# Turning the local heads' queries and keys once, by pairs of tokens, with two copies of 64 partitions

## The chip, the cores and the metric

The kernel runs on one core of one Trainium2 chip. The metric is the device time in microseconds of one execution. A core has five engines with a queue of instructions each: TensorE (PE; its weight loads are listed apart, as PEld), VectorE (DVE), ScalarE (ACT), GpSimd (POOL) and SyncE (SP, which here issues loads). Each engine works through its own queue in order and waits on semaphores that the others raise.

## The reference, cut to what matters

```python
# attention: batch 4, 8 heads, 576 tokens, 64 values a head
rel = pos[:, None] - pos[None, :]
mask_local = (rel >= 0) & (rel < 32)                    # heads 0 to 3
mask_strided = (rel >= 0) & (pos[None, :] % 32 == pos[:, None] % 32)   # heads 4 to 7
scores = np.where(masks, scale * q @ k.T, -1e9)
attn = softmax(scores)
x = (attn @ v) as 2304 rows of 512
# mixture of experts: 8 experts, each row goes to the best one
logits = x @ w_gate; e = argmax; gate = softmax(logits)[e]
out = gate * (relu(x @ w1[e]) @ w2[e])
```

## The kernel before, in words

The kernel has two phases. In the first (some 130 us) the attention is worked out, the rows x are stored and each row's expert is found. In the second each expert's rows are gathered and multiplied with its weights, with TensorE busy almost without a gap.

The attention runs as a sequence of 25 steps written out by hand (`SEQ`): 16 units of the strided heads ("z") and 9 of the local heads ("l"). A unit passes through stages: A turns queries and keys (tokens on partitions) so that the 64 values of a head stand on partitions; B multiplies them to scores, and VectorE takes the row maximum (`mx`, `mxl`) and subtracts it; ScalarE exponentiates; C turns the weights (`tp`, `tpl`) and ScalarE copies them out (`ptz`, `ptl`); D multiplies with the values (`oz`, `ol`), and VectorE divides by the sums (`smz`, then `xz` or `xl`); E turns the result for the gate. One step of the loop issues C of unit i, A of i+3, B of i+2, E of i-1, D of i, so that each engine has the work of several units in its queue.

The change is in `l_a(c, gi)`, stage A of the local heads. A chunk c is one pair of heads of one batch; its loads `lk` and `lq` lie as 96 partitions with, for each of two heads h, 6 tokens g of 64 values d: token 6p+g stands on partition p. `KTL` and `QTL` want it turned: partition 64h+d, column 6p+g. `l_a` is called 16 times, twice for each of 8 chunks, and each call makes one PSUM tile `tl` for the keys and one for the queries. Eight calls stand alone in their step ("singles" below), the other eight come two by two ("pairs"). Which step has one is set by `la_target`. The tiles `tl` share the pool `ps_t` of three banks with `tq` (strided queries and keys), `tp`, `tpl`, `tx`, `txl` and `tg`: a fourth tile waits for the bank of the first to be copied out. For the first chunk, and in some other places, `fill` issues matmuls on a constant tile (`hot`) whose results are overwritten.

Of the kernel before, what the change touches and what calls it, by code (L numbers as in the profile page):

```python
# [42 lines left out]
LE = "ss"  # L43
# [10 lines left out]
def bc(ap, axis, n):  # L54

    a = ap.unsqueeze(axis)
    shape = list(a.shape)
    shape[axis] = n
    return a.to_broadcast(shape)
# [3 lines left out]
def kernel(  # L63
# [10 lines left out]
    nc = tc.nc  # L74
# [25 lines left out]
    ident = const.tile([128, 128], F32, name="ident")  # L100
# [31 lines left out]
    with ExitStack() as p1:  # L132
# [26 lines left out]
        def fill(t, c):  # L159

            p, w = t.shape
            for _ in range(FL.count(c) if c != "*" else 1): nc.tensor.matmul(t, lhsT=hot[:, 0:p], rhs=bc(hot, 1, w // 128) if w % 128 == 0 else bc(hot[:, 0:w // 4], 1, 4), start=True, stop=True)
# [5 lines left out]
        KTL = [cp.tile([128, S], F32, name=f"ktl{i}") for i in range(4)]  # L168
        VLL = [cp.tile([128, 18, 65], F32, name=f"vll{i}") for i in range(8)]
        QTL = [cp.tile([128, S], F32, name=f"qtl{i}") for i in range(4)]  # L170
# [250 lines left out]
        def l_a(c, gi):  # L421
            for src, nm in ((lk[c], "k"), (lq[c], "q")):
                t = ps_t.tile([128, 3, 96], F32, tag="t", name="tl")
                fill(t.rearrange("p a b -> p (a b)"), nm.upper())
                if c == 0:
                    for _ in range(XF[2 * gi + (nm == "q")]):
                        fill(t.rearrange("p a b -> p (a b)"), "*")
                for i in range(3):

                    f = src.rearrange("p h g d -> p (h g d)")  # L430
                    g = 64 * (3 * gi + i)
                    nc.tensor.transpose(t[:, i, :], f[:, 320 + g:448 + g], ident[:96, :96])
                    nc.tensor.transpose(t[0:64, i, :], f[:, g:g + 64], ident[:96, :96])
                dst = QTL if nm == "q" else KTL
                {"s": nc.scalar.copy, "v": nc.vector.tensor_copy}[LE[nm == "q"]](dst[c % 4].rearrange("d (p g) -> d p g", g=6)[:, :, 3 * gi:3 * gi + 3], t.rearrange("d g p -> d p g"))

        def l_b(vv):
            s = ps_s.tile([128, 2, 512], F32, tag="s", name="sl")
# [299 lines left out]
        def emit_la(m):  # L738
            while la_done[0] < m:
                i = la_done[0]  # L740
                assert la_ok(i)
                load_to("lq", i // 2)
                l_a(i // 2, i % 2)
                la_done[0] += 1
# [302 lines left out]
    with ExitStack() as p2:  # L1047
# [184 lines left out]
        t = pools["ps_w"].tile([128, 512], F32, tag="w", name="warm2")  # L1232
# [134 lines left out]
```

## Time and profile before

| | |
|---|---|
| median of 3 runs | 380.55 us (378.71 to 381.32) |
| the profiled execution: its time | 377.83 us |
| its span, first to last instruction | 376.1 us |
| so outside the span | 1.7 us |
| mean granted TensorE clock | 0.993 of 2.4 GHz |
| busy share of the span: PE, DVE, ACT, POOL | 94%, 60%, 44%, 29% |

The busy shares are means over two phases with different limits; what the change is worth is read from the first phase. The profiled execution was 2.7 us under the median, which is as much as the three runs spread.

### The profile page before, as it was taken

The page shows a single profiled execution, that of the slowest core. Times are in us where ns is not written, and L with a number is a line of the kernel's source. Part 1 is how long each engine was busy: PE and PEld are TensorE (multiplying, and loading weights), DVE is VectorE, ACT ScalarE, POOL GpSimd, SP SyncE. Part 2 cuts the span into 40 slices and gives each one's busy share as a digit, 9 for nine tenths or more (in the row PEclk, how much of TensorE's full clock was granted, in tenths as well). Part 3 has the DMA queues.
Part 4 walks back from the last instruction along what each step waited for, and adds up shares of the span by engine and source line. Part 5 has one row for each costly group of instructions (what it writes and reads, how often), then busy time and mean ns, then how long its engine had stood idle before and what let it go on. Part 6 is the DMA issues. An engine that isn't in the chain of part 4 may idle for free. (4 is left out here: it accounts for less than half of the span.)

```text
span 376.1 us, 11209 instructions
## 1 busy us (share of the span) xinstructions
PE 354.6 (94%) x4685; PEld 321.8 (86%) x4686; DVE 224.3 (60%) x492; ACT 165.0 (44%) x301; POOL 110.0 (29%) x166
## 2 busy tenths in 40 slices
PE   7789999799998978999999999999999999999993
PEld 4678887678886647999999999999999999988992
DVE  5445664654567778445655655476576576676651
ACT  2345554355553316243435435444435535545531
POOL 4011615101653133173144024125226025030502
PEclk9999999999999989999999999999999999999998
DMA  6789969694112168999465367367467476475301
GB/s 149 165 177 198 219 169 246 161 221 106 35 62 63 59 219 234 47 287 350 161 195 185 100 196 236 118 191 227 164 218 224 126 227 226 141 256 169 108 2 59
DMA packets 59630, 62.95 MB, mean 167 GB/s; under 512 B 26077, under 2 KB 45533, under 8 KB 59570
## 3 DMA queue, kind: packets, MB, share of 16 engines
q1 hardware_dynamic: 53938, 47.75, 46.6%
q0 software_dynamic: 5632, 14.39, 13.2%
q8 instruction: 39, 0.64, 0.8%
q14 instruction: 21, 0.17, 0.1%
HBM read 52.67 MB, written 9.60 MB: 166 GB/s over the span
## 5 line engine op out<-in xcount | busy, mean ns | idle before, releaser
L1100 PE MATMUL ph<-xh,w1h 128*128 128x280 f32 (+5 forms) x252 | 78.5, 312 | 0.0
L1102 PE MATMUL ph<-xh,w1l 128*128 128x280 f32 (+5 forms) x252 | 75.4, 299 | 0.0
L1101 PE MATMUL ph<-xl,w1h 128*128 128x280 f32 (+5 forms) x252 | 75.3, 299 | 0.0
L1117 ACT ACTIVATE hh<-ph 128x280 fp32r<-128x280 f32 (+5 forms) x64 | 26.8, 419 | 95.5 <-PE ph L1102 93.6
L1118 DVE SCALAR_TENSOR_TENSOR hl<-ph,hh 128x280 fp32r<-128x280 f32 (+5 forms) x64 | 29.8, 466 | 52.3 <-ACT hh L1117 52.1
L1146 POOL DMA_INDIRECT out_dram<-yo,routing x22 | 22.7, 1030 | 128.1 <-DVE yo L1171 99.9
L1101 PE MATMUL y<-hl,w2h 128*128 128x280 f32 (+4 forms) x192 | 58.6, 305 | 0.0
L1102 PE MATMUL y<-hh,w2l 128*128 128x280 f32 (+4 forms) x192 | 58.5, 305 | 0.0
L1100 PE MATMUL y<-hh,w2h 128*128 128x280 f32 (+4 forms) x192 | 58.4, 304 | 0.0
L1080 DVE TENSOR_TENSOR w1l<-w1r,w1h 128x1024 fp32r<-128x1024 f32 x31 | 38.0, 1226 | 17.8 <-ACT w1h L1079 12.4
L1100 PEld LDWEIGHTS ph<-xh,w1h 128*128 128x128 f32 x252 | 47.6, 189 | 0.4
L1101 PEld LDWEIGHTS ph<-xl,w1h 128*128 128x128 f32 x252 | 47.7, 189 | 0.2
L1102 PEld LDWEIGHTS ph<-xh,w1l 128*128 128x128 f32 x252 | 47.5, 189 | 0.0
L1080 DVE TENSOR_TENSOR w2l<-w2r,w2h 128x1024 fp32r<-128x1024 f32 x32 | 39.2, 1224 | 10.8 <-ACT w2h L1079 10.3
L1101 PEld LDWEIGHTS y<-hl,w2h 128*128 128x128 f32 x192 | 36.1, 188 | 0.3 <-DVE hl L1118 0.3
L1100 PEld LDWEIGHTS y<-hh,w2h 128*128 128x128 f32 x192 | 36.1, 188 | 0.0
L1102 PEld LDWEIGHTS y<-hh,w2l 128*128 128x128 f32 x192 | 36.1, 188 | 0.0
L1079 ACT CAST w1h<-w1r 128x1024 fp32r<-128x1024 f32 x31 | 32.2, 1040 | 3.8 <-DMA w1r<-in_moe_w_dram 3.8
L1079 ACT CAST w2h<-w2r 128x1024 fp32r<-128x1024 f32 x32 | 33.3, 1040 | 0.1
L1183 POOL DMA_INDIRECT gt<-g_dram,routing x22 | 23.4, 1065 | 15.4 <-DMA g_dram<-GA 9.0
L125 POOL DMA_INDIRECT xg<-x_dram,routing x19 | 21.3, 1121 | 22.2 <-PE px L1090 10.3
L408 POOL DMA_DIRECT2D x_dram<-xz x16 | 11.0, 694 | 53.2 <-DVE xz L388 46.7
(211 smaller groups left out, 636.9 us busy)
## 6 DMA issues: line engine op xcount, KB each, us to landing
w1r<-in_moe_w_dram SPq DMA_DIRECT2D x32, 512.0 KB
w2r<-in_moe_w_dram SPq DMA_DIRECT2D x32, 512.0 KB
zk<-in_k_dram SPq DMA_DIRECT2D x16, 144.0 KB
zq<-in_q_dram SPq DMA_DIRECT2D x16, 144.0 KB
vzs<-in_v_dram SPq DMA_DIRECT2D x32, 72.0 KB
lk<-in_k_dram SPq DMA_DIRECT2D x16, 144.0 KB
lq<-in_q_dram SPq DMA_DIRECT2D x16, 144.0 KB
x_dram<-xz POOLq DMA_DIRECT2D x16, 144.0 KB, 3.7
```

Of the source, the lines that this page charges most:

```text
L125: nc.gpsimd.indirect_dma_start(out=t[:r], out_offset=None, in_=x_dram[:, :], in_offset=bass.IndirectOffsetOnAxis(ap=idx[:r], axis=0),)
L408: nc.gpsimd.dma_start(out=x_dram[r0:r0 + S, c0:c0 + 128].rearrange("(p g) c -> p g c", g=16)[:, 8 * gh:8 * gh + 8, :], in_=xx[64 * b:64 * ...
L1079: nc.scalar.copy(hi, t)
L1080: nc.vector.tensor_tensor(lo, t, hi.bitcast(F32), op=ALU.subtract)
L1100: nc.tensor.matmul(o, lhsT=wh, rhs=xh, start=first, stop=False)
L1101: nc.tensor.matmul(o, lhsT=wh, rhs=xl, start=False, stop=False)
L1102: nc.tensor.matmul(o, lhsT=wl, rhs=xh, start=False, stop=last)
L1117: nc.scalar.activation(hh, o, AF.Relu)
L1118: nc.vector.scalar_tensor_tensor(hl, o, 0.0, hh.bitcast(F32), op0=ALU.max, op1=ALU.subtract)
L1146: s = nc.gpsimd.indirect_dma_start(out=out[:, :], out_offset=bass.IndirectOffsetOnAxis(ap=idx, axis=0), in_=o, in_offset=None, bounds_chec ...
L1183: nc.gpsimd.indirect_dma_start(out=t[:r], out_offset=None, in_=g_dram[:, :], in_offset=bass.IndirectOffsetOnAxis(ap=idx_r(i)(j)[:r], axis=0),)
```

## The change

Before, `tl` held for three token positions g = 3 gi + i the two heads one above the other. Each position took two transposes: one of 128 columns, whose upper half is head 1, and one of 64 columns that writes head 0 over the lower half. One ScalarE copy of 128 partitions brought the tile to its columns (runs of three).

After, gi is the head. The six tokens of a head on one partition are taken as three pairs, and each pair of 128 values is turned by one transpose: token 2i stands on partitions 0 to 63, token 2i+1 on 64 to 127. Two copies then bring the halves to partitions 64 gi to 64 gi + 63: ScalarE the even tokens, VectorE the odd ones, each of 64 partitions with 288 values, to every second column.

```diff
@@ in l_a(c, gi) @@
+
+                f = src.rearrange("p h g d -> p h (g d)")
                 for i in range(3):
-
-                    f = src.rearrange("p h g d -> p (h g d)")
-                    g = 64 * (3 * gi + i)
-                    nc.tensor.transpose(t[:, i, :], f[:, 320 + g:448 + g], ident[:96, :96])
-                    nc.tensor.transpose(t[0:64, i, :], f[:, g:g + 64], ident[:96, :96])
-                dst = QTL if nm == "q" else KTL
-                {"s": nc.scalar.copy, "v": nc.vector.tensor_copy}[LE[nm == "q"]](dst[c % 4].rearrange("d (p g) -> d p g", g=6)[:, :, 3 * gi:3 * gi + 3], t.rearrange("d g p -> d p g"))
+                    nc.tensor.transpose(t[:, i, :], f[:, gi, 128 * i:128 * i + 128], ident[:96, :96])
+                dst = (QTL if nm == "q" else KTL)[c % 4].rearrange("d (p g r) -> d r p g", g=3, r=2)
+                for r in range(2):
+                    {"s": nc.scalar.copy, "v": nc.vector.tensor_copy}["sv"[r]](dst[64 * gi:64 * gi + 64, r], t[64 * r:64 * r + 64].rearrange("d g p -> d p g"))
```

What is issued changes on three engines. At the pair of calls of chunk 5 (88 us in the trace), TensorE's queue before, its first half (`tl_2024` and `tl_2032` are two tiles, `lk` and `lq` the loaded keys and queries); a name's number tells tiles apart, and `[waits X]` is the semaphore of the engine X for which the instruction waits.

```order
L432 MATMUL tl_2024<-ident_66,lk_1212 128x96 [waits PE_49]
L433 MATMUL tl_2024<-ident_66,lk_1212 64x96
L432 MATMUL tl_2024<-ident_66,lk_1212 128x96
L433 MATMUL tl_2024<-ident_66,lk_1212 64x96
L432 MATMUL tl_2024<-ident_66,lk_1212 128x96
L433 MATMUL tl_2024<-ident_66,lk_1212 64x96
L432 MATMUL tl_2032<-ident_66,lq_1215 128x96 [waits Activation_49]
```

The same place after, all four tiles and the next scores:

```order
L431 MATMUL tl_1984<-ident_66,lk_1188 128x96 [waits PE_49]
L431 MATMUL tl_1984<-ident_66,lk_1188 128x96 x2
L431 MATMUL tl_1990<-ident_66,lq_1191 128x96 [waits Activation_49]
L431 MATMUL tl_1990<-ident_66,lq_1191 128x96 x2
L431 MATMUL tl_1996<-ident_66,lk_1188 128x96 [waits Activation_49]
L431 MATMUL tl_1996<-ident_66,lk_1188 128x96 x2
L431 MATMUL tl_2002<-ident_66,lq_1191 128x96 [waits DVE_49]
L431 MATMUL tl_2002<-ident_66,lq_1191 128x96 x2
L440 LDWEIGHTS identb_71
```

Each tile has three transposes in place of six, and the fourth tile now waits for VectorE, which empties the first tile's bank last. VectorE's queue at the same place, before:

```order
L384 RECIPROCAL smz_2011<-smz_2011 100x8 [waits DVE_49]
L388 TENSOR_TENSOR xz_2014<-oz_1994,smz_2011 100x4x2x64 [waits DMASW6_49,DMASW5_49,DVE_49]
L459 TENSOR_REDUCE mxl_2091<-sl_2056 128x8 [waits PE_49]
L461 TENSOR_TENSOR pl_2093<-sl_2056,mxl_2091 128x2x4x64 [waits DVE_49]
L383 TENSOR_SCALAR smz_2121<-oz_2104 100x8 [waits PE_49]
```

and after:

```order
L388 TENSOR_TENSOR xz_1974<-oz_1954,smz_1971 100x4x2x64 [waits DMASW6_49,DMASW5_49,DVE_49]
L434 COPY ktl1_116<-tl_1984 64x288 [waits Activation_49]
L434 COPY qtl1_128<-tl_1990 64x288 [waits Activation_49]
L434 COPY ktl1_116<-tl_1996 64x288 [waits Activation_49]
L434 COPY qtl1_128<-tl_2002 64x288 [waits Activation_49]
L458 TENSOR_REDUCE mxl_2043<-sl_2008 128x8 [waits PE_49]
```

Four copies now stand ahead of the maximum `mxl`, and each waits for ScalarE, not for TensorE: the only ScalarE work that itself waits for this tile's transposes is the other half's copy. On ScalarE the row of instructions is the same as before; each `ktl` and `qtl` copy has 64 partitions in place of 128.

## Rows read from the trace of the kernel before

**Rows 1.** Windows: busy us by engine (instructions), granted clock, DMA share, GB/s.

```profile
0.00:21.00 21.00, 15.63 (x230) 10.54 (x232) 11.14 (x49) 5.76 (x13) 4.67 (x59) 1.00 0.71 165
21.00:105.00 84.00, 79.61 (x2076) 66.58 (x2077) 45.74 (x120) 43.34 (x99) 25.59 (x30) 1.00 0.75 166
105.00:131.00 26.00, 23.78 (x749) 18.95 (x737) 19.80 (x73) 9.67 (x22) 9.12 (x11) 1.00 0.18 63
131.00:376.00 245.00, 235.62 (x1656) 225.69 (x1654) 147.66 (x253) 106.20 (x169) 70.66 (x67) 0.99 0.59 179
```

**Rows 2.** Windows on tile `tl` alone: PE, PEld, ACT busy (instructions), clock, DMA.

```profile
21.70:23.50 1.80, 1.80 (x20) 1.07 (x12) 0.46 (x1) 1.00 0.80 158
26.10:28.20 2.10, 2.02 (x24) 2.01 (x24) 1.25 (x3) 1.00 0.66 131
...
80.10:81.30 1.20, 1.14 (x12) 1.00 (x12) 0.39 (x1) 1.00 1.00 254
88.10:90.20 2.10, 2.04 (x24) 1.99 (x24) 1.27 (x3) 1.00 0.11 37
97.20:99.30 2.10, 2.08 (x24) 1.99 (x24) 1.26 (x3) 1.00 0.02 8
102.50:104.60 2.10, 2.07 (x24) 1.96 (x24) 1.31 (x3) 1.00 0.06 12
```

**Rows 3.** Timeline of a single call: start, us, engine, what [idle before it].

```profile
34.74 0.49 ACT L363 COPY ptz<-tp 100x400 f32<-100x400 f32 x1
...
35.19 0.40 ACT L330 COPY qt<-tq 128x288 f32<-128x288 f32 x1
...
35.28 0.30 PE L432 MATMUL tl<-ident,lk 96*128 96x96 f32 x1
...
35.84 0.24 PE L432 MATMUL tl<-ident,lq 96*128 96x96 f32 x1
...
36.03 0.46 ACT L435 COPY ktl<-tl 128x288 f32<-128x288 f32 x1 [0.45 <-PE tl L433]
...
36.33 0.29 PE L337 MATMUL sz<-mz,identb 128*100 128x144 bf16 x2
...
37.10 0.46 DVE L348 TENSOR_REDUCE mx<-sz 100x8 f32<-100x288 f32 x1 [1.45 <-PE sz L341]
```

**Rows 4.** The same view of a pair of calls, 88 to 92 us.

```profile
88.16 0.25 PE L432 MATMUL tl<-ident,lk 96*128 96x96 f32 x1
88.19 0.69 DVE L388 TENSOR_TENSOR xz<-oz,smz 100x512 f32<-100x512 f32 x1
...
88.42 0.49 ACT L363 COPY ptz<-tp 100x400 f32<-100x400 f32 x1 [0.57 <-PE tp L361]
...
90.14 0.38 PE L441 MATMUL sl<-ml,identb 128*128 128x256 bf16 x2
```

**Rows 5.** Groups by line and form, ACT and DVE, 21 to 105 us: busy, mean ns.

```profile
L435 ACT COPY ktl<-tl 128x288 f32<-128x288 f32 x15 | 6.9, 459 | 3.6 <-PE tl L433 3.5
L413 ACT COPY xts<-tx 128x288 f32<-128x288 f32 x15 | 6.0, 399 | 19.2 <-PE tx L401 19.2
L330 DVE COPY kt<-tq 128x288 f32<-128x288 f32 x12 | 5.3, 442 | 0.0
L352 DVE TENSOR_TENSOR pzs<-sz,mx 100x288 f32<-100x288 f32 x12 | 5.5, 458 | 1.3
```

**Rows 6.** Waits of DVE, 21 to 105 us: total us, times, longest.

```profile
DVE mx L348 <- PE sz L341: 15.5, 8, 2.8
DVE mxl L459 <- PE sl L450: 11.1, 6, 2.9
```

**Rows 7.** PE timeline: two first-chunk waits for loads, and a wait at 67.86 us.

```profile
16.92 0.27 PE L432 MATMUL tl<-ident,lq 96*128 96x96 f32 x1 [0.24 <-DMA lq<-in_q_dram]
...
20.75 0.44 PE L328 MATMUL tq<-ident,zq 72*128 72x72 f32 x4 [1.22 <-DMA zq<-in_q_dram]
...
67.86 0.34 PE L450 MATMUL sl<-ktl,qtl 64*32 64x64 f32 x13 [1.66 <-issue]
```

## The prediction, made before the change was run

> **What bounds the kernel now.** I read the windows first, since the change touches only stage A of the local heads and that lies in the attention phase. From 21 to 105 us TensorE is busy 79.6 of 84 us while VectorE has 45.7 and ScalarE 43.3 [rows 1]: there TensorE's queue sets the pace, the others have half their time free. In the first 21 us it is busy 15.6, and the list of its waits there names loads [rows 7]. From 131 us on TensorE is busy 235.6 of 245, on work that the change does not touch [rows 1]; what is won before 105 us moves all of that forward. The tile `tl` alone then shows where the calls lie: eleven places hold the calls after the first, seven with 12 transposes (singles; the first has matmuls of `fill` among them) and four with 24 (pairs) [rows 2]. The first and last single and all four pairs stand there. Last I read one single and one pair instruction by instruction [rows 3, 4], because whether a shorter TensorE stretch is worth its length depends on when the three banks of `ps_t` come free.
>
> **What is removed.** A call issues 12 transposes. In the single they begin at 35.28 and the next scores at 36.33, so one takes (36.33 - 35.28) / 12 = 0.087 us; within the second tile alone it is (36.33 - 35.84) / 6 = 0.082 [rows 3]. I take 0.082. Six go from each call: 0.49 us, and 16 x 0.49 = 7.9 us in all. That a transpose of 128 columns costs more than one of 64 is excluded by those starts, which alternate at one pace. So 7.9 us is the most that TensorE can give back. The first call gives nothing: its query tile waits for a load (0.24 us) and the strided queries behind it for another (1.22 us at 20.75) [rows 7], and a load's arrival is not moved by TensorE being early. That leaves 15 x 0.49 = 7.4 us.
>
> **What is added.** ScalarE has 32 copies as before, with half the partitions and the same 288 values. The nearest rows for its price: 0.459 us for the copy as it is, 0.399 for `xts`, as many values in other runs [rows 5]. Partitions work side by side, so I take 0.46 and keep 0.40 as the other end. VectorE gets 32 new copies of 288 values out of PSUM; `kt`, the same count, takes 0.442 us and the subtraction `pzs` 0.458 [rows 5]; I take 0.44, some 14 us in all. They would be hidden in VectorE's idle time ahead of the maxima, 15.5 us in 8 waits and 11.1 in 6 between 21 and 105 us [rows 6], about 1.9 us each. But each waits for ScalarE's copy of the same tile, as the queue of the change shows. So the two halves run one after the other: a tile holds its bank for 0.46 + 0.03 + 0.44 = 0.93 us behind its transposes, where it held it 0.46. Behind VectorE's waiting copies stand the maximum, the subtraction and the division of the step, in order.
>
> **A single, worked out.** The key tile begins at 35.28, 0.05 after `ptz` ended (34.74 + 0.49) and freed its bank [rows 3]; this does not change. Its three transposes are issued by 35.53. The query tile's bank is that of `qt`, which ends at 35.59 [rows 3]; with the same 0.05 it begins at 35.64 and is issued by 35.89. The scores `sz` begin there, not at 36.33: 0.44 won, 0.05 lost to the bank. The key copy on ScalarE can begin at 35.72 (the last transpose ends 0.25 after its start, plus 0.03) and ends at 36.18, VectorE's half at 36.65; the query halves end at 36.65 and 37.12. The maximum, which could now begin at 37.10 - 0.44 = 36.66, begins at 37.13, as late as before [rows 3]. What covers that is VectorE's idle time later in the step: the divisions wait for TensorE's matmuls, and those come 0.44 earlier. So the step keeps 0.44. The same walk through the other six gives 0.34 to 0.50 (0.34 and 0.45 where a tile waits for VectorE's `kt`, 0.50 where no bank is late): 3.0 us for the seven.
>
> **A pair, worked out.** Four tiles follow each other, and three banks must turn over. Tiles one and two are issued from 88.16 to 88.65. Tile three takes the bank of `ptz`, which ends at 88.42 + 0.49 = 88.91 [rows 4]: it runs from 88.96 to 89.21. Tile four takes the bank of tile one: ScalarE's half from 88.93 to 89.39, VectorE's from 89.42 (it is free from 88.88 on, after `xz` [rows 4]) to 89.86. So tile four runs from about 89.91 to 90.16, and the scores `sl`, at 90.14 before [rows 4], begin at 90.16. Nothing is won from 24 transposes that became 12. Two more pairs (26 and 102 us) come out the same, within 0.1 us of nothing; the pair at 97 us, where tiles two and three take banks freed early by `tq`, keeps 0.35. I put the four pairs at +0.2 us together.
>
> **The sum.** 3.0 + 0.2 = 3.2 us. The profiled execution was 377.83 us with a span of 376.1; by the sum 374.6 and 372.9. The median was 2.7 us above that execution; carried over, 380.55 - 3.2 = 377.3 us.
>
> A rule of the Trainium skill bears on ScalarE's half. The trace has 0.459 us for the copy that writes runs of three values, 12 bytes of every 24, and 0.399 for `xts`, which writes runs of four [rows 5]. "SBUF — State Buffer" (its table "Specifications (TRN2)", the row on cachelines) says that accesses go by lines of 16 bytes, four fp32 values, and that at least two hits on a line are needed for full bandwidth. Runs of three every six leave lines with one hit. Every second value has two in each line, so by it the new copy would take 0.40 us, tile four of three pairs would begin 0.06 earlier, and the sum would be 3.4 us, 377.2. By the row of the copy as it is the sum stays 3.2. The two rows fit the rule; no row here writes every second value.
>
> **The rivals.** *The halves cost TensorE nothing.* If bank turnover is quicker than I have it, the most is 7.4 us: 373.2. For it: TensorE is the busy engine. Against it: rows 4, where a bank is late. A half-way case: the two halves run side by side. Then tile four of the pair would start when ScalarE's first copy ends, 89.39 + 0.05, and the scores at 89.69, 0.45 earlier; four pairs would keep about 2.1, with the singles 5.1 us: 375.4. The queue of the change, where VectorE waits for ScalarE, speaks against it. (On this the Trainium skill, "PSUM — Partial Sum Buffer", section "PSUM bank collisions raise a hardware error", says that ScalarE and VectorE may read one bank at once where their 32-partition quadrants differ, as these halves do; by it the wait is the program's and not the chip's, and side by side would be those 375.4. No run here shows two such reads.)
>
> *VectorE eats what TensorE wins.* If the late maxima pass on, because the freed score bank or the division comes late for the next step, the singles' gain goes too: 380 to 381, no change.
>
> *Slower: VectorE sets the step.* At the maxima it now idles about 1.9 us on average, 1.45 in the single shown [rows 3, 6]; a single puts 0.88 us of copies and some waiting ahead of one, a pair 1.76 and more. It decides once what is added is longer than that idle time. If half of the new 14 us is not covered, 7.0 - 3.2 = 3.8 us are lost: 384.4. Against it: idle time is longer than the addition wherever I looked.
>
> *The clock, or a fetch.* In the first 21 us TensorE's clock is at its full 2.4 GHz (1.00) although it is busy only 15.6 of 21 us [rows 1]; the change takes work out of that stretch. If it fell there to 1.2 GHz, the price is bounded by the one stretch that shows a lower mean, 0.99 of 245 us, or 2.5 us [rows 1]. And TensorE once waits 1.66 us at 67.86 for nothing that the profile shows [rows 7]; with fewer instructions ahead of it that wait can go, move or double. With such a loss on top of the sum the time is about 379.
>
> **How the numbers follow.** Chances: the forecast 0.50; halves that cost little (373 to 375.5) 0.16; eaten 0.18; slower 0.08; clock or fetch 0.08. The wait at 67.86 and the scatter of medians, whose three runs spread 2.6 us, make the forecast's own case 375.3 to 379.3. The range: below 373.6 lies about half of the cheapest rival, 0.08; above 381.4 the slower rival and a little of the eaten one, 0.11. So 373.6 to 381.4 leaves out just under 2 in 10. One per cent, 3.8 us, is about what a measurement of this kernel tells from no change: 376.7 and 384.4 are the bounds. Faster takes the cheap rivals and about 0.4 of the forecast's half: 0.36. Slower by over 1% is half of the slower rival, 0.04, and 0.05 from the upper ends of the eaten case and of the clock: 0.09. The rest, 0.55, lies within 1%.
>
> **What would show it.** Right: `tl` has 96 transposes at the old pace; VectorE's copies take about 0.44 us, their idle time ends at ScalarE's copies; in the pair near 88 us the fourth tile waits for VectorE; the maxima begin right behind the copies; windows after 131 us keep their length. Wrong: if VectorE's half starts with ScalarE's, if TensorE's idle time from 21 to 105 us, 4.4 us now, does not grow, or if waits of TensorE on `pzs`, `pl` or `xz` appear. The forecast itself fails if VectorE's copy to other partitions takes much more than 0.44 us, or if the wait at 67.86 turns into several.

## The result, and the profile after

| | before | after |
|---|---|---|
| median of 5 runs | 380.1 us (378.63 to 381.32) | 374.5 us (373.67 to 374.63) |
| the profiled execution: time, span | 377.83, 376.1 us | 373.75, 372.0 us |

The ratio is 0.9884, 95% interval 0.9847 to 0.9921: 4.4 us faster (3.0 to 5.8). The two medians are 5.6 us apart; the text goes by the ratio and its interval. A second measurement (e5 below) gave 0.9898 (0.9858 to 0.9938): 3.9 us. The forecast was 3.2 us faster, inside both intervals. Some executions take over 1.5% longer than the fastest of their kernel; ratios and medians leave them out.

**The windows** of the changed kernel answer to [rows 1] (same columns):

```profile
0.00:21.00 21.00, 16.40 (x234) 11.28 (x236) 12.54 (x54) 6.00 (x14) 4.67 (x59) 1.00 0.71 175
21.00:105.00 84.00, 78.38 (x2135) 62.38 (x2132) 61.45 (x157) 43.43 (x102) 27.27 (x32) 1.00 0.72 168
105.00:131.00 26.00, 23.42 (x624) 17.70 (x607) 20.32 (x95) 8.56 (x18) 8.31 (x11) 1.00 0.22 76
131.00:372.00 241.00, 231.09 (x1620) 222.17 (x1619) 143.88 (x220) 105.49 (x167) 68.75 (x66) 1.00 0.61 179
```

From 21 to 105 us VectorE has 61.45 us of work where it had 45.74: 13.8 us more are its 30 copies (see the prices below), the rest is later work that now falls into the same window. TensorE, which still sets the pace, is busy 78.38 of 84 us. VectorE's added work did not lengthen the program. The last row is 4 us shorter because it ends with the span, not because that work got faster: from VectorE's third `r_pe` to the last instruction it is 250.1 us before (from 126.0) and 250.8 after (from 121.2).

**A single call** in the timeline (start, us, engine), against [rows 3]:

```profile
33.63 0.47 PE L431 MATMUL tl<-ident,lk 96*128 96x96 f32 x3
...
33.98 0.47 PE L431 MATMUL tl<-ident,lq 96*128 96x96 f32 x3
34.13 0.41 ACT L434 COPY ktl<-tl 64x288 f32<-64x288 f32 x1 [0.20 <-PE tl L431]
...
34.29 0.29 PE L337 MATMUL sz<-mz,identb 128*100 128x144 bf16 x2
...
34.57 0.46 DVE L434 COPY ktl<-tl 64x288 f32<-64x288 f32 x1 [0.58 <-ACT ktl L434]
...
34.95 0.46 DVE L434 COPY qtl<-tl 64x288 f32<-64x288 f32 x1
...
35.44 0.46 DVE L348 TENSOR_REDUCE mx<-sz 100x8 f32<-100x288 f32 x1
```

The scores `sz` begin 0.66 us after the first transpose (34.29 - 33.63), where they began 1.04 after it. VectorE's half waits for ScalarE's half of the same tile, and the maximum follows 1.81 us after the first transpose, as late as before (37.10 - 35.28 = 1.82): what VectorE got to do lies in the idle time that it had.

**A pair**, same view, against [rows 4]:

```profile
83.74 0.41 PE L431 MATMUL tl<-ident,lk 96*128 96x96 f32 x3
...
84.00 0.49 ACT L363 COPY ptz<-tp 100x400 f32<-100x400 f32 x1 [0.57 <-PE tp L361]
...
84.38 0.41 ACT L434 COPY ktl<-tl 64x288 f32<-64x288 f32 x1
84.54 0.28 PEld L431 LDWEIGHTS tl<-ident,lk 96*128 96x128 f32 x3 [0.33 <-ACT ptz L363]
...
84.83 0.46 DVE L434 COPY ktl<-tl 64x288 f32<-64x288 f32 x1 [0.36 <-ACT ktl L434]
...
85.35 0.47 PE L431 MATMUL tl<-ident,lq 96*128 96x96 f32 x3 [0.34 <-DVE ktl L434]
...
85.65 0.38 PE L440 MATMUL sl<-ml,identb 128*128 128x256 bf16 x2
```

Tile four begins 0.06 us after VectorE emptied tile one (84.83 + 0.46 = 85.29), and `sl` 1.91 us after the first transpose, where it took 1.98: of 12 transposes saved, 0.07 us are left. The same wait stands at all four pairs; the list of TensorE's waits from 21 to 105 us has it as one row:

```profile
PE tl L431 <- DVE ktl L434: 1.4, 4, 0.4
```

**Prices** (groups by line and form, 21 to 105 us: busy, mean ns), against [rows 5]:

```profile
L434 DVE COPY ktl<-tl 64x288 f32<-64x288 f32 x15 | 6.9, 461 | 8.2 <-ACT ktl L434 8.1
L434 DVE COPY qtl<-tl 64x288 f32<-64x288 f32 x15 | 6.9, 457 | 1.1 <-ACT qtl L434 0.5
...
L434 ACT COPY qtl<-tl 64x288 f32<-64x288 f32 x15 | 6.3, 421 | 1.9 <-PE tl L431 1.9
...
L434 ACT COPY ktl<-tl 64x288 f32<-64x288 f32 x15 | 6.2, 410 | 1.9 <-PE tl L431 1.6
```

**VectorE's waits** from 21 to 105 us (total us, times, longest), against [rows 6]:

```profile
DVE ktl L434 <- ACT ktl L434: 8.1, 11, 2.3
...
DVE mx L348 <- PE sz L341: 1.9, 1, 1.9
DVE mxl L458 <- PE sl L449: 1.8, 3, 0.7
```

The idle time ahead of the maxima, 26.6 us before, is 3.7: the copies and their waits for ScalarE stand there now. TensorE's wait of 1.66 us at 67.86 [rows 7] has no counterpart in this execution; what that means took experiments.

### The profile page after: what moved, and what is told of

Its sections match the earlier page's. It is cut to its first block, busy times and chain, and to the rows that moved or that the text cites. A ratio compares the mean times of both kernels' runs of the same rounds, so it can differ in the third digit from the quotient of the medians.

```text
span 372.0 us, 11043 instructions
## 1 busy us (share of the span) xinstructions
PE 349.3 (94%) x4589; PEld 313.5 (84%) x4590; DVE 238.2 (64%) x524; ACT 163.5 (44%) x301; POOL 109.0 (29%) x166
## 3 DMA queue, kind: packets, MB, share of 16 engines
q0 software_dynamic: 5632, 14.39, 13.8%
## 5 line engine op out<-in xcount | busy, mean ns | idle before, releaser
L125 POOL DMA_INDIRECT xg<-x_dram,routing x19 | 20.2, 1066 | 21.6 <-PE px L1089 10.6
```

Source lines behind the costliest of these rows:

```text
L125: nc.gpsimd.indirect_dma_start(out=t[:r], out_offset=None, in_=x_dram[:, :], in_offset=bass.IndirectOffsetOnAxis(ap=idx[:r], axis=0),)
```

## The experiments

The theory: **bank turnover**. TensorE gives back what the three banks of `ps_t` allow, 3.2 us; VectorE's copies cost nothing but the time that they hold a bank. The rivals: VectorE's 14 us cost by themselves; what a place wins is lost at the next wait; and, for what the first comparison shows beyond 3.2 us, that the change removes TensorE's wait at 67.86.

All runs are read by one measure: the time from a place's first transpose to TensorE's next other work, from the timelines. It came out the same within 0.05 us in the profiles of one kernel, apart from places before 25 us, where loads land early or late, and from two into which a wait for nothing that the profile shows fell (near 52 us in e1 and e11). The times at the head of the table are those of the kernel before. In us:

| kernel | six singles, 35 to 82 us, summed | pairs at 26, 88, 97, 102 us | pairs summed | pairs against before |
|---|---|---|---|---|
| before | 6.22 | 1.98, 1.98, 2.04, 1.98 | 7.98 | |
| the change | 3.95 | 1.91, 1.91, 1.78, 1.95 | 7.55 | 0.43 won |
| halves side by side (e2) | 3.94 | 1.59, 1.64, 1.34, 1.61 | 6.18 | 1.80 won |
| transposes alone (e3) | 4.30 | 1.43, 1.43, 1.28, 1.46 | 5.60 | 2.38 won |
| copies alone (e4) | 6.23 | 2.21, 2.22, 2.27, 2.22 | 8.92 | 0.94 lost |
| by tile (e7) | 3.94 | 1.84, 1.84, 1.71, 1.88 | 7.27 | 0.71 won |
| both on ScalarE (e8) | 3.94 | 1.84, 1.84, 1.70, 1.88 | 7.26 | 0.72 won |

Singles win 6.22 - 3.95 = 2.27. The seventh, near 22 us, wins 0.49 between the first profiles of the two kernels (1.73 to 1.24): with the pairs 3.19 us. It repeats least of all: the three later profiles of before have 1.96 there and those of the change 1.71 to 1.72, so it wins 0.25 and the sum is 2.95 us. What makes the difference is a wait for the bank that VectorE's `kt` empties, here from TensorE's waits in e5:

```profile
PE tl L162 <- DVE kt L330: 0.3, 1, 0.3
```

(The 4.30 of e3 has one place of 1.01 near 44 us; its others are as in the change.)

**e1, the kernel before again**, unchanged.

> The kernel before, profiled a second time. Theory A (the twelve places with calls give 3.2 us, the rest of the 5.6 us between the medians is waits that the kernel before has and the changed one has not): the wait of 1.66 us on no visible cause near 67.9 us, the load wait near 20.7 us and the stretch of half clock in the second phase appear again, at about the same places, span 375 to 378 us. Rival B (that execution was an odd one): the wait near 67.9 us is gone or under 0.5 us, span about 374 us, and the calls must then be worth more than the timelines show.

379.51 us, span 377.8. The places of calls after 25 us take what they took, but for the one near 52 us. A wait of TensorE for nothing that the profile shows, 1.7 us long, stands near 53 us; near 70 us there is one of 0.3 us. Half clock (TensorE at 1.2 GHz) stands from 12 to 19 us and not near 138 us. So the span came as theory A had it, and the wait near 67.9 us went as rival B had it.

**e2, the halves side by side.** The program is told that the two copies of a tile touch different columns and partitions, so VectorE no longer waits for ScalarE:

```diff
-                for r in range(2):
-                    {"s": nc.scalar.copy, "v": nc.vector.tensor_copy}["sv"[r]](dst[...], t[...])
+                cs_ = [{"s": nc.scalar.copy, "v": nc.vector.tensor_copy}["sv"[r]](dst[...], t[...]) for r in range(2)]
+                tc.declare_no_dep(cs_[1].ins, cs_[0].ins, reason="disjoint columns and partitions")
```

> The changed kernel, with VectorE's half no longer waiting for ScalarE's half of the same tile (the bytes written are disjoint, the bytes read lie in different partitions). Theory A (the pairs of calls gain nothing because the bank of the first tile is held by two copies in turn): the fourth tile of a pair begins about 0.4 us earlier behind the third, three pairs keep 0.4 us each more, the single calls are unchanged; 1.2 to 2.0 us faster than the changed kernel, ratio to before about 0.984. Rival C (the two reads of one bank slow each other, or the pairs are bound by something else): copies longer than 0.5 us or no gain, ratio 0.988.

373.37 us (372.56 to 375.32), ratio 0.9872 (0.9798 to 0.9946): with an interval of 2.0 to 7.6 us below before, the time can't tell this kernel from the change, and the places have to. The pair near 88 us in the timeline:

```profile
86.70 0.41 PE L431 MATMUL tl<-ident,lk 96*128 96x96 f32 x3
...
87.35 0.42 ACT L433 COPY ktl<-tl 64x288 f32<-64x288 f32 x1
87.46 0.46 DVE L433 COPY ktl<-tl 64x288 f32<-64x288 f32 x1
...
88.03 0.28 PEld L431 LDWEIGHTS tl<-ident,lq 96*128 96x128 f32 x3 [0.25 <-ACT ktl L433]
88.06 0.44 PE L431 MATMUL tl<-ident,lq 96*128 96x96 f32 x3
...
88.34 0.38 PE L440 MATMUL sl<-ml,identb 128*128 128x256 bf16 x2
```

The two copies read one bank at the same time, at 0.42 and 0.46 us, no slower than one behind the other. Tile four begins 1.36 us after tile one (88.06 - 86.70), in the change 1.61, and the pairs win 1.80 us in place of 0.43. So what costs the pairs most of their gain is that the two copies run one behind the other.

**e3, the transposes alone.** One ScalarE copy of 128 partitions per tile; it writes every second column, so that half of the tokens land on the wrong partitions and columns and the scores are of other values:

```diff
-                for r in range(2):
-                    {"s": nc.scalar.copy, "v": nc.vector.tensor_copy}["sv"[r]](dst[64 * gi:64 * gi + 64, r], t[64 * r:64 * r + 64].rearrange("d g p -> d p g"))
+                nc.scalar.copy(dst[:, gi], t.rearrange("d g p -> d p g"))
```

> The new transposes alone: one ScalarE copy of 128 partitions for each tile, as before the change, and nothing on VectorE; the odd tokens land in the other head's rows, so the attention of the local heads is not the reference's. Theory A: the bank of a tile is held for one copy of 0.41 us; singles as in the changed kernel (3.0 us), three pairs about 0.45 us better each: ratio to before about 0.984, as in the kernel with the halves side by side. Rival D (VectorE's new 14 us cost something by themselves): clearly faster than the halves side by side, by 1 us or more.

372.76 us (370.63 to 374.02), ratio 0.9849 (0.9766 to 0.9933). Its groups from 21 to 105 us have the price of that copy, and its timeline has the pair:

```profile
L433 ACT COPY ktl<-tl 128x288 f32<-128x288 f32 x15 | 6.3, 420 | 2.2 <-PE tl L431 2.0
```

```profile
86.72 0.41 PE L431 MATMUL tl<-ident,lk 96*128 96x96 f32 x3
...
87.52 0.28 PEld L431 LDWEIGHTS tl<-ident,lk 96*128 96x128 f32 x3 [0.33 <-ACT ptz L363]
...
87.84 0.47 PE L431 MATMUL tl<-ident,lq 96*128 96x96 f32 x3
88.03 0.41 ACT L433 COPY ktl<-tl 128x288 f32<-128x288 f32 x1
...
88.14 0.38 PE L439 MATMUL sl<-ml,identb 128*128 128x256 bf16 x2
```

With VectorE out of it a pair keeps 0.55 of its 0.98 us; most of the rest is the bank of tile three, which waits for `ptz` as in the change. With one copy per tile, then, three banks let through 2.27 + 0.49 + 2.38 = 5.1 us (4.9 by the later profiles of the place near 22 us), not 7.4. The time is 0.6 us below e2's, less than the intervals can tell; the 1 us by which rival D was to show itself was not seen.

**e4, the copies alone.** Twelve transposes per call as before, with the two copies of the change behind them (they bring values of other tokens to the columns):

```diff
-                dst = QTL if nm == "q" else KTL
-                {"s": nc.scalar.copy, "v": nc.vector.tensor_copy}[LE[nm == "q"]](...)
+                dst = (QTL if nm == "q" else KTL)[c % 4].rearrange("d (p g r) -> d r p g", g=3, r=2)
+                for r in range(2):
+                    {"s": nc.scalar.copy, "v": nc.vector.tensor_copy}["sv"[r]](dst[64 * gi:64 * gi + 64, r], t[64 * r:64 * r + 64].rearrange("d g p -> d p g"))
```

> The new copies alone: the twelve old transposes of a call, then the two copies of 64 partitions in turn; the columns are then not those of the tokens, so the attention of the local heads is not the reference's. Theory A: TensorE spends 0.49 us on a tile, so a bank is late only in the pairs, by about 0.2 us each; 0.5 to 1 us slower than before, ratio 1.001 to 1.003. Rival D: the 14 us on VectorE delay maxima and divisions at every call, 3 us slower or more, ratio over 1.008.

377.65 us (376.55 to 379.97), ratio 1.0006 (0.9968 to 1.0045). The pair near 88 us:

```profile
88.30 0.42 ACT L436 COPY ktl<-tl 64x288 f32<-64x288 f32 x1
...
88.76 0.46 DVE L436 COPY ktl<-tl 64x288 f32<-64x288 f32 x1 [0.43 <-ACT ktl L436]
...
89.27 0.30 PE L432 MATMUL tl<-ident,lq 96*128 96x96 f32 x1
...
89.82 0.38 PE L442 MATMUL sl<-ml,identb 128*128 128x256 bf16 x2
```

VectorE's 14 us by themselves cost 0.94 us at the pairs, through the bank, and nothing at the singles. The rival by which VectorE sets the step would have lost 3 us or more here, with no transposes saved; the interval ends at 1.7 us, and the rival falls.

**e5, the change again**, with e6 to e8 on another chip.

> The changed kernel once more, to see which parts of its profile repeat. Bank turnover (my theory): the eleven places of calls begin their next work 3.2 us earlier in sum than in the profile before, singles 0.3 to 0.5 each, pairs within 0.3 of nothing, and the time is 3 to 5 us below before, ratio 0.987 to 0.993. The rest of the 4.8 us that the first profile of the change was ahead of before at 125 us (loads that landed about 1 us earlier, no wait of 1.66 us for nothing that the profile shows) belongs to single executions: by that, this profile may have such a wait of 1.6 to 1.7 us somewhere from 45 to 70 us, and stretches of half clock of 3.4 us, as the runs e1 to e3 had. Rival: the change itself removes that wait; then it is absent here as well.

373.55 us (372.19 to 375.99), ratio 0.9898 (0.9858 to 0.9938). The places after 25 us take what they took; the one near 22 us has 1.72. TensorE has no wait over 0.5 us for nothing that the profile shows: the rival is left standing here, and e9 to e12 take it up.

**e6, the halves side by side again.**

> The half-copies side by side, once more, beside the change on one chip. Bank turnover: pairs keep 1.8 us as in e2, where the change keeps 0.45, so this kernel is 1.3 us faster than the change of this call, ratio to before 0.983 to 0.990. Rival (what a pair wins is lost at the next wait): pairs keep 1.8 us at their own place, but the time equals the change's within 0.5 us.

373.79 us (371.72 to 376.63), ratio 0.9909 (0.9875 to 0.9942). The pairs win 1.76 us, as in e2, and from a pair to the next place TensorE takes as long as in the change: 7.12 us behind the pair near 26 us (7.13 in the change), 7.08 in e2 behind the one near 88 (7.09 in the change). Once only, near 97 us in e6, 0.8 us goes there, 0.6 of it a wait for nothing that the profile shows. So in the trace nothing is lost at the next wait. But a time 1.3 us below the change's was not seen: the two medians are 0.2 us apart, which is the rival's sign, and the intervals of the two, each 2.5 to 3 us wide, allow the 1.3 us only at their edges. Shown is the gain at the places; that it reaches the end was not shown.

**e7, by tile.** Both halves of the key tile on ScalarE, both of the query tile on VectorE:

```diff
-                    {"s": nc.scalar.copy, "v": nc.vector.tensor_copy}["sv"[r]](...)
+                    {"s": nc.scalar.copy, "v": nc.vector.tensor_copy}["sv"[nm == "q"]](...)
```

> Both halves of the key tile on ScalarE, both of the query tile on VectorE; no copy waits for another engine. Bank turnover: a tile's bank is held for two copies in a row as in the change (0.41 + 0.41 on ScalarE against 0.41 + 0.04 + 0.46), so the fourth tile of a pair still waits, for ScalarE now, 0.05 to 0.1 us less each; singles win as in the change; the time equals the change's within 1 us. Rival (the wait between the engines is the cost, not the length of the two copies): pairs gain as in the run with the halves side by side, 0.35 to 0.7 each, and the time is 1.3 us below the change's. Second rival (maxima come earlier because VectorE is not held by ScalarE, and this shortens the steps): 1 to 2 us below the change's.

374.62 us (371.77 to 377.14), ratio 0.9916 (0.9885 to 0.9947): the change's time within noise. The pair near 91 us:

```profile
91.67 1.70 ACT L434 COPY ktl<-tl 64x288 f32<-64x288 f32 x4
...
92.56 0.47 PE L431 MATMUL tl<-ident,lq 96*128 96x96 f32 x3 [0.27 <-ACT ktl L434]
```

No copy waits for another engine, and tile four still waits: 0.27 us in place of 0.34, the 0.05 to 0.1 less that was expected. It is the length of two copies in a row that holds the bank, whoever makes them. (This profiled execution ran at half clock from 55 to 61 us; the pairs lie outside of it.)

**e8, both halves on ScalarE.**

```diff
-                    {"s": nc.scalar.copy, "v": nc.vector.tensor_copy}["sv"[r]](...)
+                    {"s": nc.scalar.copy, "v": nc.vector.tensor_copy}["ss"[r]](...)
```

> Both halves of every tile on ScalarE; VectorE is as before the change. ScalarE gets 32 copies more of about 0.41 us, 13 us in all. Bank turnover: singles keep their 0.3 to 0.5; in a pair ScalarE has eight copies in a row, tile four begins 0.82 us after tile one's first copy started and so as in the change or 0.1 earlier, but the copies end only 3.4 us after the first started, and what is queued behind them on ScalarE (exponentials, copies of turned weights) comes 1 us late: the time is that of the change or up to 2 us above. Rival (VectorE's 14 us are what costs, hidden in the change by chance): 1 us or more below the change. Rival (ScalarE becomes the bound of these steps): no gain over before.

375.69 us (374.94 to 377.73), ratio 0.995 (0.9921 to 0.9979): 1.9 us below before, some 2 us above the change. Its six singles and four pairs win 3.0 us (the one near 22 us lies in a stretch of half clock and can't be compared); part of that goes again at a wait that the change has at 0.2 us in all. The first row of TensorE's waits from 30 to 131 us:

```profile
PE tg L539 <- ACT xtl L514: 2.0, 4, 0.8
```

ScalarE's queue, with 13 us more, delivers `xtl` late. VectorE freed of 14 us brings nothing: the second run against the rival that VectorE costs by itself.

**e9 to e12, two further profiles each of before (e9, e11) and of the change (e10, e12)**, all unchanged.

> A further profile of the kernel before. Two of its profiles had a wait of TensorE of 1.66 to 1.7 us for nothing that the profile shows, at 67.86 in one and near 50 us in the other; the two of the changed kernel had none over 0.5 us from 21 to 105 us. If such waits belong to single executions, this profile has one at yet another place or none, and its eleven places of calls take the same 1.04 (singles) and 1.98 (pairs) us to the next work as before. Rival (the wait belongs to the longer queue of transposes, and the change removes it): a wait of 1.6 to 1.7 us stands here again between 45 and 70 us.

> A further profile of the changed kernel, beside the last one. If waits of 1.6 to 1.7 us for nothing that the profile shows belong to single executions, one may stand here; the eleven places take 0.66 (singles) and 1.91 (pairs) us to the next work, as in its first two profiles. Rival (the change removes it): none over 0.6 us from 21 to 105 us.

> The kernel before once more, for the same count: a wait of 1.6 to 1.7 us between 45 and 70 us speaks for the rival (it belongs to the longer queue), none speaks for waits of single executions.

> The changed kernel once more, for the same count: a wait of 1.6 to 1.7 us for nothing that the profile shows speaks for waits of single executions, none leaves the rival standing. Either way the places of the calls take what they took in its first profile, within 0.05 us, load waits ahead of 25 us excepted.

377.49 and 379.05 us for before, 377.94 and 376.75 for the change. From TensorE's waits, 21 to 105 us, the row of before (e9), then the rows of the change (e10):

```profile
PE sl L450 <- issue: 0.9, 1, 0.9
```

```profile
PE oz L377 <- issue: 1.8, 1, 1.8
...
PE tx L401 <- issue: 1.1, 1, 1.1
```

Here the change has the long waits (1.4 us in e12, too) and the kernel before has none over 0.9 us (0.8 in e11). The rival that the change removes them falls. How long such a wait is belongs to the single execution, but where it stands does not. Counted along TensorE's records in the trace (matmuls, weight loads and its sequencer's), the one near 68 us is at record 2754 in every profile of both kernels: 1.66, 0.28, 0.92 and 0.55 us in the four of before, 0.15, 0.52, 1.80 and 1.42 in those of the change. The one near 53 us is at record 1987. With fewer transposes ahead of it, record 2754 is a later instruction: `sl` L450 before, `oz` L377 in the change. So the wait moved along the program, and its length varies in both kernels alike. Half clock, too, comes and goes: 3.4 us of it stand at 138 us in the profile of before and in e11, near 137 us in e10 and e12, and not there in the first two profiles of the change. From four profiles each the mean span is 376.7 us (376.1, 377.8, 375.7, 377.3) before and 374.1 (372.0, 373.4, 376.1, 375.0) after: 2.6 us apart, with single ones of one kernel up to 4.1 apart. On the one chip of e9 to e12 the two times of each kernel average 378.3 and 377.3 us, 0.9 apart: so few executions can't confirm a difference of 3 us, nor refute it.

## Why the prediction was right

**The sum.** 3.2 us was forecast, and the places give 3.19 in the first profile. That they agree so closely is luck in part: singles were put at 3.0 and gave 2.76, pairs at 0.2 and gave 0.43. By the later profiles, where the place near 22 us wins less, the sum is 2.95. The measured 4.4 and 3.9 us lie above, by less than their intervals allow. The first profile of the change was 4.8 us ahead at 125 us, 1.6 more than the sum, because that one execution had no long wait as at 67.86 (1.66 us) and a load that landed 1.1 us earlier, less some smaller waits of its own. At the end 4.1 us were left: a stretch of half clock in the profile of before (3.4 us at 138 us) put the change 5.8 us ahead, and then 1.6 us went again, 1.2 of them in a wait for gathered rows that the profile of before does not have:

```profile
PE px L1089 <- DMA xg<-x_dram,routing: 1.2, 1, 1.2
```

(e5 has 0.4 us there, e9, which is before, 0.8.) I can't tell a rest of some 1 us from nothing.

By the bounds that the prediction set itself the agreement is weaker. Its forecast's own case was 375.3 to 379.3 us; the median after is 374.5, which lies in the band of the rival *halves that cost little* (373 to 375.5) and below 376.7, where it had put a chance of 0.36, with 0.55 on a time within 1%. That rival is refuted at the pairs all the same, so the mechanism is read from the places and not from the time.

**A single.** The order of events came as worked out: the query tile's transposes begin 0.35 us behind the key tile's (forecast 0.36), and the maximum is as late as before. The mis-sized term: three transposes that begin after a wait take 0.31 us to the next work (33.98 to 34.29), not 0.25, so a single keeps 0.38 and not 0.44. The 0.25 was read where transposes follow transposes (it is 83.99 - 83.74 in the pair). The six singles after 25 us keep 0.29 to 0.49, where 0.34 to 0.50 was forecast.

**A pair.** Tile three begins 0.80 us after tile one (84.54 - 83.74), as forecast. Tile four was to begin 1.75 after it and did at 1.61. ScalarE's half began 0.13 earlier than I had it: at 84.38, while `ptz` is drawn to 84.49. I had let copies on one engine follow end to end, but a next one starts up to 0.11 us before the drawn end. The half also took 0.41 us, not 0.46; VectorE's took 0.46, not 0.44. So three of the four pairs kept 0.03 to 0.07 instead of about nothing; the one near 97 us kept 0.26, not 0.35.

**ScalarE's price.** Forecast 0.46, with 0.40 as the other end; measured 0.410 for keys, 0.421 for queries. e3 separates the two things that changed: with 128 partitions and every second column it was 0.420 for keys. So the columns made it cheaper, not the 64 partitions. (The Trainium skill, "SBUF — State Buffer", table "Specifications (TRN2)", row on cachelines, asks for at least two hits on each 16-byte line for full bandwidth, which every second value has. The trace agrees, with 0.41 to 0.42 in place of 0.459.)

**The rivals.** Halves that cost nothing: refuted by the wait at every pair, and e3 lowers what was possible with one copy per tile from 7.4 to 5.1 us. Side by side: not what the change does; e2 did it and its places gave 4.6 us (forecast 5.1). (For two engines in one bank, the Trainium skill, "PSUM — Partial Sum Buffer", section "PSUM bank collisions raise a hardware error", allows it where the 32-partition quadrants differ; e2 agrees, 0.42 and 0.46 us at once.) VectorE eats the gain, or sets the step: e4 and e8 against it, and where no load or stray wait falls between two places, the time between them is as before to 0.01 us (3.67 between the last two singles in both kernels). The clock or a fetch: such losses come and go in both kernels; half clock of 3.4 us and more stands somewhere from 12 to 19 us in e1, e9 and e11 (before) and in e5, e10 and e12 (the change), and in neither of the first two profiles. In e1 and e11 it is 6.9 us long, up to 3.4 us of TensorE's work by an estimate, more than the 2.5 that the prediction took as the bound.

**The signs.** All that were named for right came: 96 transposes at the old pace ((83.99 - 83.74) / 3 = 0.083 us each), VectorE's copies at 0.46 us behind ScalarE's, the fourth tile's wait for VectorE, and the maximum right behind the copies (34.95 + 0.46 = 35.41; `mx` at 35.44). The work after 131 us kept its length to 0.8 us. Of those for wrong none did: TensorE's idle time from 21 to 105 us grew, from 4.4 to 5.6 us, and it has no new wait on `pzs`, `pl` or `xz`.

## What to carry to other kernels

When an engine's work is shortened, count what it can use by the turnover of the buffers behind it: here half of the transposes went, 7.9 us by the forecast's price, and some 3 us of that came through at the places, with a bank held for two copies in a row. Two copies that share a tile should be looked at in the queue for a wait of one for the other. Here they wrote different columns and read different partitions, and did not need it; without it the pairs won 1.80 in place of 0.43 us. (Why the program had the wait, whether for the interleaved columns or for another reason, was not tried.) And a difference between two single profiles is to be read place by place before it is believed: lengths of the changed places after 25 us repeated to 0.05 us, whole spans of one kernel only to 4.

## What the runs showed of the hardware

Successive copies of one engine overlap in the trace: `ktl` starts at 84.38 while `ptz` on the same engine lasts to 84.49.

ScalarE's copy of 288 values took 0.459 us in runs of three every six, and 0.41 to 0.42 in every second value, with 64 or 128 partitions; VectorE took 0.46 for the same.

Two copies out of one bank at the same time, ScalarE's from partitions 0 to 63 and VectorE's from 64 to 127, took 0.42 and 0.46 us, as long as one behind the other (e2).

TensorE has, in half of the profiles, a wait of 0.8 to 1.8 us with no releaser from 50 to 70 us. It stands at the same count of TensorE's records in the trace, whatever the instruction there: at 1987 in e1 and e11 (`tl`), e3 and e10 (`tx`), at 2754 in before and e9 (`sl`), e10 and e12 (`oz`). The other waits of its matmuls with no releaser, those over 0.14 us from 24 to 125 us, are at 963, 1219, 4290, 5058 and 5315. All seven counts lie multiples of 256 apart, to within one. The length varies from one execution to the next, from 0.15 to 1.80 us at 2754. (In e2, e7 and e8 the list names `pzs` for a wait of 1.1 to 1.7 us at 1987; in e2 `pzs` had been done for 0.4 us.) What these waits are was not tried.
